# Six roundings of weights held behind the first layer, and the stores of raw weight quarters held back, in an attention and feed-forward kernel

## The chip, the cores and the metric

One core of one Trainium2 chip. The metric is the device time of one execution in microseconds (us), lower is better.

Engines are written as in the profile: PE (matrix multiplication), ACT, DVE, POOL (the three engines for elementwise work), and SP, which in this kernel issues nearly all transfers between DRAM and the chip. PSUM is the memory that PE's products go to; a bank is the part of it that one product takes up here. The granted clock is the share of full speed at which the profile shows PE's clock. L872 means line 872 of the kernel. **The change inserts four lines early on, so L872 of the kernel before is L876 in the changed kernel**, and so with all lines after the first inserted ones.

## The reference

```python
# q, k, v: (8, 8, 576, 64) float32;  w_ch1: (512, 2048), w_ch2: (2048, 512), both float64
q_s = softmax(q, axis=-1);  k_s = softmax(k, axis=2)
kv  = einsum('bhsd,bhse->bhde', k_s, v)
x   = einsum('bhsd,bhde->bhse', q_s, kv)          # -> (8, 576, 512), heads side by side
u   = x + real(fft2(x, axes=(1, 2)))
un  = (u - mean(u)) / sqrt(var(u) + 1e-6)         # over the last axis
out = u + maximum(un @ w_ch1, 0) @ w_ch2
```

(The two softmax lines stand for the reference's own six lines.) The weights arrive as float64, that is as pairs of 32-bit words, and the kernel rounds them to float32 itself.

## The kernel before

The kernel works through the token groups, and for each does attention, the Fourier mix, a normalisation and the two layers of the feed-forward block. For all groups but the first, the two layers are *split*: the weight matrices are cut into quarters, sums and differences of quarters are formed once (the *combination*), and seven products take the place of eight. The sums are stored to DRAM and read back. The first group cannot wait for that. It goes through *plain* layers, while the weights are still being rounded. This is the stretch from about 60 to 205 us, and the change lies entirely in it.

The weights are rounded in 32 blocks, 0 to 15 for the first layer and 16 to 31 for the second. Each block is loaded as 512 KB of words, and rounded by ACT, DVE, DVE, ACT and POOL in turn:

```python
def convert(i):
    pair = raws.pop(i).rearrange("p (n w) -> p n w", w=2)
    lo, hi = pair[:, :, 0], pair[:, :, 1]
    # ... cut: out is the block's place in the weights
    n = ("bc", "bb", "bc", "bb")[i] if i < 4 else "acc"
    if i < 20:
        t = self.ps.tile([P, 512], F32, tag=n, name=n, bufs=3 if i >= 4 else 1)[:]   # PSUM
    else:
        t = hi.bitcast(F32)                                                           # in place
    # ... cut
    nc.scalar.activation(t, hi.bitcast(F32), ACT.Copy, scale=2.0 ** -112)                            # L347
    V.tensor_scalar(out=to.bitcast(I32), in0=ti, scalar1=3, ..., op0=ALU.logical_shift_left)         # L348
    V.scalar_tensor_tensor(out=to.bitcast(I32), in0=ti, scalar=-(1 << 31), in1=to.bitcast(I32), ...) # L349
    nc.scalar.activation(lo, lo.bitcast(U32), ACT.Copy, scale=2.0 ** -29)                            # L352
    nc.gpsimd.tensor_tensor(out=out.bitcast(I32), in0=to.bitcast(I32), in1=lo, op=ALU.add)           # L353
```

There are only 14 places for words, so a block's words are overwritten by those of a later block. `WORDS_AT` gives the place of each block. The load of the later one is issued right behind the rounding of the earlier one, and waits for it:

```python
WORDS_AT = [*range(8), 8, 9, 10, *range(3, 8), 0, 1, 2, 8, 9, 10, 4, 5, 6, 7, 8, 11, 12, 7, 13, 8]
LATE_WORDS = (27, 28, 30)          # these have places of their own, and are loaded after the first layer

def round_blocks(some):
    for i in some:
        convert(i)
        if i in after:             # after[25] = 29, after[26] = 31, ...
            fetch(after[i])
```

The plain layers, and the order in which everything is issued around them:

```python
def up(f):                                     # first layer, block f of 16; three PSUM banks in turn
    n = ("ba", "bb", "bc")[f % 3]
    ph = self.ps.tile([P, 512], F32, tag=n, name=n)
    for k in range(KT):
        nc.tensor.matmul(ph[:], lhsT=self.w1sb[:, f, k * P:(k + 1) * P], rhs=..., ...)   # L872
    nc.scalar.activation(h[:, f, :], ph[:], ACT.Relu)                                    # L874
```
```python
round_blocks(range(1))
blk.gate(unT[:, 0, 0, :], blk.raws[NF][0:1, 0:2])
round_blocks(range(1, 4))
n = 2 * NF - 16
turn = [2 * i if i < 4 else 3 * i - 4 for i in range(12)]
for f in range(NF):                            # NF = 16
    up[f]()
    free(f)
    round_blocks(range(4 + n * f // NF, 4 + n * (f + 1) // NF))
rest = [lambda i=i: round_blocks([i]) for i in range(4 + n, 2 * NF)]
# ... cut: the steps of the combination; the loads of q; the words of LATE_WORDS
for i in range(len(down)):                     # the second layer, 64 steps on PE (L881)
    down[i]()
    if i in turn:
        rest[turn.index(i)]()
    # ... cut: a share of the combination, of the second batch's attention and of its transform
```

The second batch's attention runs between the matmuls of the second layer. The *q turn* is one step of it: PE transposes a tile of q (L613), ACT copies it out of PSUM (`qT`, L620), PE multiplies it by kv (L645), and ACT copies the result to x (L647). There are four such tiles.

Two helpers order work without moving data. `gate(t, raw)` is a DVE instruction of 1x2 elements (L490). It writes the first two words of `raw` back unchanged, but reads `t` too, so that nothing that uses `raw` can be placed ahead of what makes `t`. `hold` and `free(f)` do the same with tiny copies behind the relu of block `f`: the q loads may go out after block 12.

## Time and profile before

| | before |
|---|---|
| median of three runs | 1134.09 us (1133.23 to 1135.87) |
| span of the profiled execution (that run took 1136.19 us) | 1134.4 us |
| busy share of PE, DVE, ACT, POOL | 96%, 48%, 36%, 30% |
| second block of the first layer starts | 68.43 us |
| second layer starts | 129.71 us |
| split layers start | 204.44 us |

PE is the bound. The busy share of 96% is an average, however. The view that cuts the span into stretches tells where the other 4% lie. Its columns are: the stretch, its length, then the busy time and number of groups of PE, of its weight loads, of DVE, ACT and POOL, then the mean granted clock of PE, the share of the DMA engines and GB/s. Two stretches of the kernel before:

```profile
110.00:130.00 20.00, 12.79 (x25) 5.65 (x26) 6.99 (x15) 10.81 (x30) 4.99 (x7) 0.83 0.52 168
130.00:205.00 75.00, 73.01 (x271) 40.75 (x270) 52.24 (x115) 26.24 (x65) 35.36 (x38) 1.00 0.72 251
```

PE lost 7.2 us of the 20 us around block 13 and ran the rest at a granted clock of 0.83. In the second layer it lost 2.0 us of 75.

### The profile page before, as it was taken

What the parts mean: (1) busy time and instruction counts of PE and PEld (TensorE: products, weight loads), DVE (VectorE), ACT (ScalarE), POOL (GpSimd) and SP (SyncE); (2) the same over time, 40 slices, a digit from 0 to 9 for tenths busy, and PEclk for the clock granted to TensorE, in tenths of its full rate; (3) what the DMA queues carried; (4) which work ended last, traced back from release to release, by engine and by line L of the source; (5) the groups of instructions that cost most, each with busy time, mean ns of one, the idle gap of its engine ahead of it and who ended that gap; (6) DMA issues with size and microseconds to landing.
All of it is one profiled execution on the core that took longest, in us unless ns stands there. A gap on an engine that the chain in (4) does not pass through costs nothing.

```text
span 1134.4 us, 14587 instructions
## 1 busy us (share of the span) xinstructions
PE 1094.5 (96%) x5440; PEld 915.5 (81%) x5440; DVE 542.3 (48%) x1109; ACT 404.3 (36%) x975; POOL 335.3 (30%) x304
## 2 busy tenths in 40 slices
PE   5798899999999999999999999999999999999997
PEld 4643355888888988898889888888889888888886
DVE  6776586368433734375344733583434352203201
ACT  6694423355333513362325322442334152201200
POOL 2065382226103510334023402261034203302320
PEclk9999899999999999999999999999999999999999
DMA  9556668354346534544356335552453344434441
GB/s 304 174 200 186 231 218 303 116 206 176 111 151 220 185 142 145 194 157 176 127 176 220 149 102 179 193 200 107 144 193 148 116 156 156 182 143 156 151 186 55
DMA packets 92581, 193.79 MB, mean 171 GB/s; under 512 B 23120, under 2 KB 59728, under 8 KB 85344
## 3 DMA queue, kind: packets, MB, share of 16 engines
q1 hardware_dynamic: 90712, 191.82, 49.2%
q10 hardware_dynamic: 1800, 1.05, 0.3%
q8 instruction: 43, 0.70, 0.2%
q14 instruction: 26, 0.21, 0.1%
HBM read 168.72 MB, written 28.31 MB: 174 GB/s over the span
## 4 chain that ended last, share of the span: by engine, by line
PE 86%; ACT 4%; DMA 3%; DVE 3%; issue 2%; POOL 1%; ACTq 0%; SPq 0%; POOLq 0%; DVEq 0%
PE bb L942 15%; PE bb L980 15%; PE ba L942 10%; PE bc L980 10%; PE bc L942 10%; PE ba L980 10%; PE acc L563 3%; PE acc L645 2%; PE acc L738 2%; PE acc L741 2%; PE acc L762 2%; PE tr L613 1%; PE tr L842 1%; PE bc L881 1%; PE tr L549 1%
## 5 line engine op out<-in xcount | busy, mean ns | idle before, releaser
L942 PE MATMUL bb<-unT,big 128*128 128x256 f32 x768 | 187.4, 381 | 0.0
L980 PE MATMUL bb<-big 128*128 128x256 f32 x768 | 172.1, 379 | 0.0
L942 PEld LDWEIGHTS bb<-unT,big 128*128 128x128 f32 x768 | 142.8, 190 | 23.6 <-DVE u L910 2.6
L980 PEld LDWEIGHTS bb<-big 128*128 128x128 f32 x768 | 145.4, 190 | 20.3
L359 POOL TENSOR_TENSOR big<-big 128x512 f32<-128x512 f32 (+1 forms) x38 | 46.2, 1217 | 305.9 <-ACT big L954 305.9
L942 PE MATMUL bc<-unT,big 128*128 128x256 f32 x512 | 125.4, 379 | 0.0
L954 ACT ACTIVATE big<-big 128x512 f32<-128x512 f32 x96 | 60.3, 629 | 182.6 <-DVE big L953 182.1
L942 PE MATMUL ba<-unT,big 128*128 128x256 f32 x512 | 123.6, 379 | 0.2 <-ACT unT L846 0.2
L980 PE MATMUL bc<-big 128*128 128x256 f32 x512 | 116.0, 379 | 0.5 <-DVE x L997 0.5
L980 PE MATMUL ba<-big 128*128 128x256 f32 x512 | 114.8, 379 | 0.0
L914 DVE TENSOR_TENSOR u<-bb,s 128x512 f32<-128x512 f32 x40 | 27.6, 691 | 177.8 <-PE bb L980 120.4
L980 PEld LDWEIGHTS bc<-big 128*128 128x128 f32 x512 | 96.1, 190 | 14.3 <-DVE x L997 0.9
L980 PEld LDWEIGHTS ba<-big 128*128 128x128 f32 x512 | 95.7, 190 | 12.1
L942 PEld LDWEIGHTS bc<-unT,big 128*128 128x128 f32 x512 | 95.1, 190 | 12.6
L942 PEld LDWEIGHTS ba<-unT,big 128*128 128x128 f32 x512 | 95.1, 190 | 12.2 <-ACT unT L846 0.5
L367 POOL TENSOR_TENSOR unT<-unT 128x512 f32<-128x512 f32 x8 | 14.2, 1774 | 182.1 <-DVE unT L366 182.1
L602 ACT ACTIVATE q<-q,qm 128x64 f32<-128x64 f32 x240 | 61.6, 339 | 6.1 <-DVE qm L600 6.0
L910 DVE TENSOR_TENSOR u<-bb,s 128x512 f32<-128x512 f32 x40 | 27.6, 690 | 73.3 <-PE bb L942 38.7
L953 DVE TENSOR_TENSOR big<-bc,u 128x512 f32<-128x512 f32 x64 | 44.1, 689 | 22.8 <-PE bc L942 21.7
L992 POOL TENSOR_TENSOR x<-x,u 128x512 f32<-128x512 f32 x14 | 17.7, 1267 | 113.9 <-DVE u L914 101.3
L846 ACT COPY unT<-tr 128x512 f32<-128x512 f32 x36 | 20.7, 586 | 79.7 <-PE tr L842 79.1
L953 DVE TENSOR_TENSOR big<-bb,s 128x512 f32<-128x512 f32 x32 | 22.1, 690 | 55.6 <-PE bb L942 55.5
(248 smaller groups left out, 1653.9 us busy)
## 6 DMA issues: line engine op xcount, KB each, us to landing
big<-w1s SPq DMA_DIRECT2D x64, 896.0 KB
big<-w2s SPq DMA_DIRECT2D x56, 1024.0 KB
big<-in_w_dram SPq DMA_DIRECT2D x21, 512.0 KB
q<-in_q_dram SPq DMA_DIRECT2D x27, 256.0 KB
k<-in_kT_dram SPq DMA_DIRECT2D x24, 288.0 KB
v<-in_v_dram SPq DMA_DIRECT2D x24, 256.0 KB
words<-in_w_dram SPq DMA_DIRECT2D x8, 512.0 KB
mirror<-x SPq DMA_DIRECT2D x14, 256.0 KB
```

What stands on the lines that cost most here:

```text
L359: e1.tensor_tensor(out=to(4), in0=at(2), in1=at(3), op=ALU.add)
L563: nc.tensor.matmul(pk, lhsT=ks[:, c, :], rhs=v[:, c, :], start=(c == 0), stop=(c == NC - 1))
L602: nc.scalar.activation(heads[:, h, :], heads[:, h, :], ACT.Exp, bias=m[:, h:h + 1])
L645: nc.tensor.matmul(px[:, r * P:(r + 1) * P], lhsT=qT[:, r, :], rhs=self.kvr[b % 2][:, r, :], start=True, stop=True)
L738: nc.tensor.matmul(full[:, at:at + size], lhsT=t[:, own], rhs=self.ft[:, f + at:f + at + size], start=at == 0, stop=False, skip_group_chec ...
L741: nc.tensor.matmul(full[:, 0:NM], lhsT=g[:, tail], rhs=self.ft[:, f:f + NM], start=False, stop=True, skip_group_check=True)
L910: V.tensor_tensor(out=temp("u2"), in0=box["bb"][:], in1=box["s1"][:], op=ALU.add)
L914: V.tensor_tensor(out=temp("u3"), in0=box["bb"][:], in1=box["s1"][:], op=ALU.add)
L942: nc.tensor.matmul(bank()[:, i, :], lhsT=w[:, WA_AT[m], k * P:(k + 1) * P], rhs=unT[:, B_AT[m], k, :], start=first and i == 0 and k == 0, ...
L953: V.tensor_tensor(out=hp(i), in0=bank[:], in1=u[:], op=ALU.add)
L954: nc.scalar.activation(hp(i), hp(i), ACT.Relu)
L980: nc.tensor.matmul(bank()[:, i, :], lhsT=h[p][:, A_AT[m], i * P:(i + 1) * P], rhs=w[:, p, :], start=first and i == 0 and p == 0, stop=p == ...
```

## The change

The intent is to take the roundings that are not urgent out of the way of the first layer's relus. In the order of the code, 26 blocks instead of 20 are rounded by its end, with their halves through PSUM. The order on each engine is settled when the program is built, and differs: in the trace of the kernel before, POOL had finished 29 of the 32 blocks by then, all but 27, 28 and 30. So three roundings really leave the first layer, those of 26, 29 and 31. Block 26 is gated to the last relu, and blocks 27 to 31 to the first x of the second batch. The stores of raw quarters are held until block 12 by two tiny copies.

```diff
@@ free(f) @@
             for t in held.get(f, ()):
                 copy(t, self.h0[0:1, f, 0:1])
+            if f == 12:
+                for w in (self.w1sb[0:1, :, HD::HD], self.w2sb[0:1, 0:4, ::HD]):
+                    copy(w, w)
@@ convert(i) @@
-            if i < 20:
+            if i < 26:
@@ the first group @@
-            n = 2 * NF - 16
-            turn = [2 * i if i < 4 else 3 * i - 4 for i in range(12)]
+            n = 2 * NF - 10
             for f in range(NF):
                 up[f]()
                 free(f)
                 round_blocks(range(4 + n * f // NF, 4 + n * (f + 1) // NF))
+            blk.gate(blk.h0[:, NF - 1, :], blk.raws[26][0:1, 0:2])
+            turn = (0, 16, 19, 21, 23, 25)
@@ the second layer @@
                 down[i]()
+                if i == turn[1]:
+                    for n in range(27, 32):
+                        blk.gate(blk.xpart(1, 0, 0), blk.raws[n][0:1, 0:2])
                 if i in turn:
                     rest[turn.index(i)]()
```

## The prediction

> **What bounds the kernel now.** I read first the page's busy shares (the matmul engine is busy 96% of the span), then the waits of PE in two stretches, then PE, ACT and SP in order of time around the one large wait. From 205 us to the end PE waits for 2.4 us in all: nothing is to be gained there. From 60 to 205 us, where the first batch goes through the unsplit layers and the weights are rounded, the waits of PE are:
>
> ```profile
> PE bb L872 <- ACT big L874: 7.4, 1, 7.4
> PE acc L738 <- ACT ZT L749: 1.1, 1, 1.1
> PE ba L872 <- ACT unT L846: 1.0, 1, 1.0
> ...
> PE acc L645 <- ACT qT L620: 0.6, 1, 0.6
> ```
>
> Columns: total us, times, longest. One wait is 7.4 us. PE in order of time shows where it lies and what it costs besides:
>
> ```profile
> 102.77 3.60 PE L872 MATMUL bc<-unT,big 128*128 128x512 f32 x8
> 106.20 3.60 PE L872 MATMUL ba<-unT,big 128*128 128x512 f32 x8
> 117.21 5.80 PE L872 MATMUL bb<-unT,big 128*128 128x512 f32 x8 [7.41 <-ACT big L874]
> 122.84 3.60 PE L872 MATMUL bc<-unT,big 128*128 128x512 f32 x8
> 126.27 3.60 PE L872 MATMUL ba<-unT,big 128*128 128x512 f32 x8
> ```
>
> These are blocks 11 to 15 of the first layer (L872, three PSUM banks in turn). Block 13 could have started at 109.63 (106.20 + 3.43, the start-to-start time of the others), starts at 117.21 and takes 5.63 instead of 3.43. The second layer then begins at 129.71. Block 13 waits for its bank, which the relu (L874) of block 10 has to empty. That block's matmuls ended at 102.8, so I ask what ACT did instead:
>
> ```profile
> 101.12 0.58 ACT L874 ACTIVATE big<-ba 128x512 f32<-128x512 f32 x1
> 111.53 0.65 ACT L347 ACTIVATE big<-big 128x512 f32<-128x512 f32 x1 [9.82 <-DMA big<-in_w_dram]
> 112.09 0.66 ACT L352 ACTIVATE big<-big 128x512 int32<-128x512 uint32 x1
> 115.38 0.65 ACT L347 ACTIVATE words<-words 128x512 f32<-128x512 f32 x1 [2.63 <-DMA words<-in_w_dram]
> 115.94 0.66 ACT L352 ACTIVATE words<-words 128x512 int32<-128x512 uint32 x1
> 116.49 0.57 ACT L874 ACTIVATE big<-bb 128x512 f32<-128x512 f32 x1
> ```
>
> Two roundings stand ahead of the relu in ACT's order, and both wait for words from DRAM. Their loads, on the SP queue:
>
> ```profile
> 107.98 0.33 SPq L328 DMA_DIRECT2D big<-in_w_dram  x1
> 110.04 0.33 SPq L328 DMA_DIRECT2D words<-in_w_dram  x1
> ```
>
> By the places that the kernel gives to words these are blocks 29 and 31: each overwrites the words of blocks 25 and 26, whose last rounding steps on POOL end at 107.96 and 110.01. So work of the second layer (block 29 is first multiplied after 168 us) stands in front of a relu that PE needs at 109.6. It is an order, not a lack of capacity: ACT idles 9.8 us there.
>
> **What the Trainium skill says.** (1) "TensorE: Matmul & The Clock Gate", Architectural detail: the queues of ACT and DVE are strict FIFO, and PE alone pulls weight loads ahead. The trace agrees: the relu ran 13.7 us after its matmuls, right behind the two roundings. (2) The same page, Part 1 (The HAM clock gate): after an idle window of about 3.4 us the array runs at half clock until it has been busy for about as long. The trace agrees: block 13 took 2.20 us longer, and the mean granted clock from 109.8 to 129.7 was 0.83. So the wait costs more than its 7.4 us. (3) "SBUF — State Buffer", SBUF: two separate sides: DVE and GpSimd share a port pair under an exclusive lock, and the loser waits. (4) "VectorE: DVE Perf Modes", Why PSUM operands drop a tier: a PSUM operand rules the two-port mode out. The trace agrees on both: the shift (L348) took 686 ns on average from PSUM, but from 415 to 1509 ns from the words in SBUF, the long ones beside POOL.
>
> **The change part by part.** The order of the built programs shows PE's 864 rows unchanged; only ACT, DVE, POOL and SP differ.
>
> *Five gates of late words to the second batch's first x, and one of block 26 to the last relu.* Each is a DVE instruction of 1x2 elements, 0.14 us by those already there; six cost 0.9 us of DVE and nothing on the path. They do the work: in ACT's new order the relus of blocks 9 to 13 follow one another with no rounding between, block 26 stands behind the last relu, and 27 to 31 behind the first x copy (L647). What is then left from 109.63 to the second layer is three blocks of 3.43 = 10.29 us, against 129.71 - 109.63 = 20.08 now. **Saved: 9.8 us** (7.6 wait, 2.2 slow clock).
>
> *26 blocks instead of 20 with their halves through PSUM.* No instruction more. Blocks 20 to 25 read PSUM, 0.69 us per shift instead of about 1 us on average. ACT must now wait for one of three banks. By DVE's new order I place block 22 off its bank at about 99.2 (block 20 starts at 94.07 as now, since it needs POOL's block 18; then one copy that needs POOL's block 19, at 95.4; then six steps of 0.6). ACT then does block 25 and the relu of block 8 at about 100.5; PE needs that bank at 102.77. Slack 2.3 us: no wait.
>
> *The two copies of the held quarters.* 1x16 and 1x8 elements, 0.17 us each. The one on the first weights must follow the matmuls of block 12 that read the column (about 108.8), and block 13's third matmul must follow the copy; that matmul comes at 111.3, so 2 us are spare. The quarters' stores (8 of 128 KB) move from 87-96 us to about 109. They are wanted only when the split layer's weights are read back after 160 us: hidden. The q loads, gated to block 12's relu, go out at about 111 instead of 119.3.
>
> *Moved behind the first layer.* Blocks 26, 29 and 31 join 27, 28 and 30 in the second layer: three more roundings, each about 1.3 us of POOL, 1.1 of ACT, 1.1 of DVE, so 3.9, 3.4 and 3.4 us. POOL is busy 36 of the 74.7 us there, ACT 26, DVE 53: room, if the order is kind. Deadlines, 9.8 us earlier than now: block 26 at 148.4, 27 at 149.3, 28 at 158.8. Ready, estimated: first x copy 136.7, gates about 138.5, then ACT one block per 1.12 us and POOL one per 1.3: 27 at 141-142, 31 at 147-150. All in time; ACT's copies of later q and x for PE stand between these roundings, and may cost PE 0 to 1 us.
>
> *What the first layer's combination wins.* It starts with the last block of the first layer (127.58 now, so 117.8), and in POOL's new order blocks 27 and 28 no longer stand in its middle (141.58, 146.64), so it should end some 15 to 20 us earlier than now, the next keys' load goes out before 155 rather than at 165.8, and the 1.15 us wait at L738, which comes from those keys (landed 177.15) standing ahead of ZT on ACT, should vanish. I count 0.8 for it.
>
> Sum: 9.8 + 0.8 - 0.8 (new small waits, estimated) = 9.8 us; 1134.1 - 9.8 = **1124.3 us**.
>
> **Rivals.** (a) *The gain is given back in the second layer*: the chain of waits from 118 to 181 us runs through POOL, DVE and DMA, not PE, and ended with a PE wait already; with PE 9.8 us ahead and 3.9 us more of POOL work, that chain would keep up to 4-6 us. For it: that chain. Against: all of it starts at the end of the first layer too, and its POOL order gets better. It would make 1128 to 1130. (b) *Rounding through PSUM makes ACT wait for DVE in the first layer*: a relu of blocks 4 to 8 late by more than its slack, or PE held by the new copy. For it: ACT and DVE are 71% and 77% busy from 63 to 109.8. Each is worth 1 to 3 us: 1126 to 1127. (c) *The words held now arrive late and PE waits for block 26 or 27*: the slack is 7 us or more by my placing, but four chained estimates stand behind it; 1126 to 1132 if so. (d) *Everything fits and other waits go too*: the 0.6 us wait at L645 as well, 1122.
>
> **Range and chances.** Most weight lies on 1122 to 1126, with a tail upward from (a) and (c); the runs scatter by 2.6 us. Range 1121 to 1129.5. Two per cent are 22.7 us, over twice all that PE waits for in this stretch, so faster by that is all but excluded (0.01); slower by that would need the second layer to stall for over 30 us (0.02); within 0.97.
>
> **What would show it.** Right: PE has no wait over 1 us in L872 after its first block, block 13 takes 3.4 us, the second layer begins at 119.5 to 120.5, and the split layer (204.44 now) begins at 193 to 195.5. ACT's relu of block 10 starts within 1 us of its matmuls' end. The roundings 27 to 31 run from about 138 to 146 on ACT. Wrong: a new wait of PE for POOL's L353 group or for qT in the second layer (rivals a, c), a wait at L872 on DVE's copy or a late relu (b), or a first matmul of the split layer that waits for its loads.

## The result, and the profile after

| | before | after |
|---|---|---|
| median of four runs each, one chip | 1133.89 us (1133.23 to 1135.87) | 1129.21 us (1128.49 to 1129.27) |
| ratio | | 0.9954, 95% interval 0.9937 to 0.9972 |
| span of the profiled execution | 1134.4 us | 1126.7 us |

A ratio is the mean time of one kernel's fast runs over that of the other's fast runs of the same rounds, so it is not quite the ratio of the medians in the table. The change is 4.7 us faster by the medians. The time lies within the predicted range, 0.3 us below its upper end, but the gain is half of the 9.8 us that were worked out. The range held because of the tail that was left for rival (a), and not because of the sum.

The first layer behaved as foreseen. PE of the changed kernel in order of time, blocks 13 to 15 and the start of the second layer:

```profile
106.94 3.60 PE L876 MATMUL bb<-unT,big 128*128 128x512 f32 x8
110.37 3.60 PE L876 MATMUL bc<-unT,big 128*128 128x512 f32 x8
113.81 3.60 PE L876 MATMUL ba<-unT,big 128*128 128x512 f32 x8
117.24 3.60 PE L885 MATMUL bc<-big 128*128 128x512 f32 x8
```

Every block starts 3.43 us after the one before it. The 7.41 us wait is gone, and so is the slow clock behind it. ACT's relus of blocks 11 and 12 in the changed kernel show why:

```profile
103.71 0.60 ACT L878 ACTIVATE big<-bc 128x512 f32<-128x512 f32 x1 [2.83 <-PE bc L876]
107.14 0.60 ACT L878 ACTIVATE big<-ba 128x512 f32<-128x512 f32 x1 [2.84 <-PE ba L876]
```

ACT now waits for PE, and not PE for ACT: no rounding stands between these relus.

From 60 to 205 us the waits of PE in the changed kernel are (total us, times, longest):

```profile
PE acc L649 <- ACT qT L624: 4.4, 1, 4.4
PE ba L876 <- ACT unT L850: 1.0, 1, 1.0
...
PE acc L742 <- ACT ZT L753: 0.2, 1, 0.2
```

The wait for ZT has almost vanished, as foreseen (but not for the reason foreseen, see below). **The wait for qT, 0.6 us before, is now 4.4 us.** The stretches of the changed kernel that answer to those shown of before say the same:

```profile
110.00:130.00 20.00, 20.00 (x51) 9.09 (x50) 15.07 (x34) 11.21 (x36) 9.83 (x11) 1.00 0.66 226
130.00:205.00 75.00, 70.24 (x276) 43.50 (x275) 54.77 (x105) 25.82 (x58) 33.48 (x34) 0.98 0.69 238
```

PE is busy for all of the first 20 us at full clock. In the next 75 us it now loses 4.8 us instead of 2.0, and the clock falls to 0.98.

To add this up, I count from the start of the first layer's second block, whose matmuls are the same work at full clock in every run:

| stretch | before | after | difference |
|---|---|---|---|
| second block to second layer | 129.71 - 68.43 = 61.28 | 117.24 - 65.74 = 51.50 | -9.78 |
| second layer to split layers | 204.44 - 129.71 = 74.73 | 196.10 - 117.24 = 78.86 | +4.13 |
| split layers to the end | 1134.4 - 204.44 = 929.96 | 1126.7 - 196.10 = 930.60 | +0.64 |
| sum | 1065.97 | 1060.96 | -5.01 |

-5.0 us agrees with the medians (-4.7 here, -5.2 in a later repetition). The two profiled executions differ by 7.7 us. The other 2.7 us lie before the second block, 1.7 of them in the first block: it took 5.37 us in the one and 3.67 us in the other, for the same work. Over all profiles it took 5.37 us in six and 3.67 us in seven. Both kernels that I profiled twice showed the same value twice, and what decides between the two stayed open. I leave this part out of every comparison.

Next, the new wait. The changed kernel has several chains on several engines here. PE first, then ACT:

```profile
143.75 2.08 PE L649 MATMUL acc<-kvr,qT 128*128 128x128 f32 x8 [4.37 <-ACT qT L624]
145.62 1.06 PE L617 MATMUL tr<-ident,spare 128*128 128x128 f32 x4
```
```profile
139.32 0.67 ACT L351 ACTIVATE spare<-spare 128x512 f32<-128x512 f32 x1 [5.66 <-DVE spare L494]
...
142.66 0.56 ACT L651 COPY x<-acc 128x512 f32<-128x512 f32 x1
143.13 0.57 ACT L624 COPY qT<-tr 128x512 f32<-128x512 f32 x1
```

The cut lines are the other five steps of the roundings of blocks 27, 28 and 29. ACT idled 5.66 us until DVE had passed the gate (L494), then did three roundings, and only then the copy of qT that PE was waiting for. After the wait PE also ran at a slow clock: the two groups took 1.87 and 0.86 us from start to start, against 0.89 and 0.44 us at full clock. The excess is 0.98 + 0.42 = 1.40 us, and 1.46 with the next group.

DVE passed the gate at 139.14, though the x that it stands for was copied by ACT at 132.58 to 133.16. DVE had work of the combination ahead of it in its queue, and that waited for POOL. DVE, then POOL:

```profile
136.10 0.93 DVE L365 TENSOR_TENSOR big<-big 128x256 f32<-128x256 f32 x1 [1.98 <-POOL big L363]
...
139.14 0.21 DVE L494 SCALAR_TENSOR_TENSOR spare<-x,spare 1x2 int32<-1x2 int32 x2
```
```profile
125.67 1.36 POOL L357 TENSOR_TENSOR big<-big,words 128x512 int32<-128x512 int32 x1 [2.09 <-issue]
132.93 0.91 POOL L371 TENSOR_TENSOR s<-big 128x256 f32<-128x256 f32 x1 [5.89 <-issue]
```

POOL finished block 26 at 127.03, and then stood still for 5.89 us. Its next step overwrites the temporary `s`, which a store has to have read first. So the SP queue comes into it:

```profile
119.11 1.43 SPq L332 DMA_DIRECT2D spare<-in_w_dram  x3
127.06 0.33 SPq L332 DMA_DIRECT2D words<-in_w_dram  x1
127.44 0.43 SPq L409 DMA_DIRECT2D w1s<-u  x1
127.91 0.43 SPq L409 DMA_DIRECT2D w1s<-s  x1
```

Between 120.54 and 127.06 SP issued nothing. At its head stood the load of block 31's words, which overwrite those of block 26, and block 26 is now gated behind the last relu. That gate was late as well: the relu ended at 118.08, but DVE reached the gate only at 122.21, behind other work. The stores of `u` and `s` stood behind it. A load that nobody wants before some 20 us later held up the stores that the combination needs. This is the reading of one trace. The experiments test it.

### The profile page after: what moved, and what is told of

It is laid out like the page before. It is cut to its first block, busy times and chain, and to the rows that moved or that the text cites.

```text
span 1126.7 us, 14593 instructions
## 1 busy us (share of the span) xinstructions
PE 1092.0 (97%) x5440; PEld 917.6 (81%) x5440; DVE 542.3 (48%) x1117; ACT 404.6 (36%) x975; POOL 333.7 (30%) x304
## 4 chain that ended last, share of the span: by engine, by line
PE 84%; DVE 3%; issue 2%; POOL 2%; ACT 1%; DMA 0%; POOLq 0%; ACTq 0%; DVEq 0%
PE bb L946 15%; PE bb L984 15%; PE bc L984 10%; PE ba L984 10%; PE bc L946 10%; PE ba L946 10%; PE acc L567 2%; PE acc L649 2%; PE bc L885 2%; PE acc L766 1%; PE acc L742 1%; PE acc L745 1%; PE tr L846 1%; PE tr L617 1%; PE tr L553 1%
## 5 line engine op out<-in xcount | busy, mean ns | idle before, releaser
L946 PE MATMUL bb<-unT,big 128*128 128x256 f32 x768 | 187.4, 382 | 0.7 <-DVE u L918 0.7
L946 PEld LDWEIGHTS bb<-unT,big 128*128 128x128 f32 x768 | 143.2, 190 | 24.0 <-DVE u L914 2.6
L946 PE MATMUL bc<-unT,big 128*128 128x256 f32 x512 | 125.5, 380 | 0.0
L946 PE MATMUL ba<-unT,big 128*128 128x256 f32 x512 | 123.6, 380 | 0.2 <-ACT unT L850 0.2
L946 PEld LDWEIGHTS bc<-unT,big 128*128 128x128 f32 x512 | 95.4, 191 | 12.4
L946 PEld LDWEIGHTS ba<-unT,big 128*128 128x128 f32 x512 | 95.3, 191 | 12.0 <-ACT unT L850 0.5
```

What stands on the lines that cost most here:

```text
L946: nc.tensor.matmul(bank()[:, i, :], lhsT=w[:, WA_AT[m], k * P:(k + 1) * P], rhs=unT[:, B_AT[m], k, :], start=first and i == 0 and k == 0, ...
```

## The experiments

**Theory.** The new wait has two causes that add up. (1) The load of 31 holds SP, so the gates come late. (2) Once the gates open, three roundings of blocks that are not urgent stand on ACT ahead of qT. **Rivals**: the gates wait for DVE or POOL work anyway, whatever SP does; or the second layer is bound by the chain through POOL, DVE and DMA, so that the time would come back elsewhere (rival (a) of the prediction); or other parts of the change (more blocks by PSUM, the hold) cost something.

All runs agreed with the reference. In the table all times are medians. "Layer 1" is from the second block to the second layer, "layer 2" from there to the split layers, both from the profiles (us). The time before was 1134.58, 1134.79 and 1134.67 us in the three calls (11 runs each). Kernels of one call ran on one chip.

| call | kernel | us | ratio to before (95%) | layer 1 | layer 2 |
|---|---|---|---|---|---|
| | before (first profile) | | | 61.28 | 74.73 |
| | the change (first profile) | | | 51.50 | 78.86 |
| 1 | fetch31_later | 1127.32 | 0.9937 (0.9926 to 0.9949) | 51.50 | 76.61 |
| 1 | gates_alone | 1131.52 | 0.9977 (0.9966 to 0.9989) | 54.48 | 80.05 |
| 1 | hold_alone | 1134.64 | 1.0004 (0.9990 to 1.0018) | 60.90 | 73.24 |
| 1 | no_late_gates | 1132.12 | 0.9984 (0.9969 to 0.9999) | 53.37 | 80.40 |
| 2 | late_gates_last_x | 1130.06 | 0.9950 (0.9937 to 0.9963) | 51.50 | 78.95 |
| 2 | late_gates_last_x_sp_held | 1132.71 | 0.9980 (0.9967 to 0.9994) | 51.50 | 82.61 |
| 2 | no_gate_on_26 | 1129.15 | 0.9944 (0.9932 to 0.9956) | 52.32 | 79.49 |
| 2 | gates_29_31 | 1131.16 | 0.9968 (0.9953 to 0.9983) | 51.50 | 81.05 |
| 3 | last_x_all_at_once | 1125.89 | 0.9925 (0.9911 to 0.9938) | 51.50 | 76.35 |
| 3 | change_again | 1129.50 | 0.9959 (0.9945 to 0.9973) | 51.50 | 78.84 |
| 3 | fetch31_again | 1126.05 | 0.9928 (0.9915 to 0.9941) | 51.50 | 76.61 |

### 1. The load of block 31 issued later (fetch31_later)

The change, but the load of 31 is issued at step 12 of the second layer, behind the stores:

```diff
-            if i in after:
+            if i in after and after[i] != 31:
                 fetch(after[i])
@@ the second layer @@
                 down[i]()
+                if i == 12:
+                    fetch(31)
```

> The change, except that the load of block 31's words is issued at job 12 of the second layer instead of right after block 26's rounding. Theory (the load of 31 holds the SP queue from 120.5 to 127.1 us while it waits for block 26, the stores of the second quarter pair go out 6 us late, GpSimd's combination, VectorE's gates and ScalarE's roundings follow late, and PE waits 4.4 us for qT and loses 1.5 us more at a slow clock): GpSimd's wait of 5.9 us before the first L371 falls under 1.5 us, the gates run 4 to 5 us earlier, PE's wait for qT falls to under 1 us, and the time is 4 to 6 us under that of the change: 1123.5 to 1125.5. Rival 1 (the gates stand too late in VectorE's order whatever the stores do, behind the combination): the wait stays at 3 to 4.5 us and the time at 1128 to 1130. Rival 2 (GpSimd and VectorE simply have too much work there): the wait moves to another instruction, time 1127 to 1130.

POOL, DVE and PE of this kernel:

```profile
129.87 0.93 POOL L371 TENSOR_TENSOR s<-big 128x256 f32<-128x256 f32 x1 [0.62 <-DMA w1s<-s]
```
```profile
139.15 0.21 DVE L494 SCALAR_TENSOR_TENSOR spare<-x,spare 1x2 int32<-1x2 int32 x2
```
```profile
143.81 1.16 PE L649 MATMUL acc<-kvr,qT 128*128 128x128 f32 x8 [2.21 <-ACT qT L624]
144.81 0.82 PE L617 MATMUL tr<-ident,spare 128*128 128x128 f32 x4
145.42 3.40 PE L885 MATMUL ba<-big 128*128 128x512 f32 x4
```

POOL's wait fell from 5.89 to 0.62 us, so the place of that load was its cause. Two things came together: counted from the start of the second layer, the store of `s` was issued 3.6 us earlier (at +7.05 instead of +10.67), and POOL could go on 3.4 us after that instead of 5.0, now that no load of 512 KB had been issued just before. The gates opened 19.69 us after the start of the second layer (119.46) instead of 21.90, and the qT wait fell by as much, from 4.37 to 2.21 us. The expectation of a wait of 1 us or less was **missed**, and so was the time (1123.5 to 1125.5 expected, 1127.32 measured). DVE still did eight steps of the combination, from 134.97 to 139.15, ahead of the gates. The slow clock stayed too: the four matmuls at 145.42 take 1.88 us at full clock. So the theory holds for cause (1), at half of the wait.

### 2. The five gates alone (gates_alone)

The kernel before, with the five gates at step 16 and nothing else:

```diff
                 down[i]()
+                if i == 16:
+                    for n in range(27, 32):
+                        blk.gate(blk.xpart(1, 0, 0), blk.raws[n][0:1, 0:2])
```

> The kernel before plus only the five gates of the words of 27 to 31 (20 blocks rounded as before, no hold of stores, no gate on 26). Block 26 is rounded in the first layer here, so 31's load is not held and does not hold the SP queue. Theory (the wait at block 13 of the first layer comes from the roundings of 29 and 31 in front of a relu): that wait is gone, 9.8 us saved there; and no wait for qT over 1.5 us: 1123.5 to 1126, so better than the whole change. Rival (the other two parts are needed for the first layer): a wait of several us at L872 stays, 1129 to 1134. Rival (the gates themselves cost the qT wait): the first layer is clean but qT waits 3 to 4.5 us: 1128 to 1130.

The expectation was wrong. The wait at block 13 vanished (blocks 10 to 15 start 3.43 us apart), but two new waits came. PE of this kernel:

```profile
120.99 3.67 PE L881 MATMUL bc<-big 128*128 128x512 f32 x8 [2.82 <-POOL s L360]
...
147.69 2.08 PE L645 MATMUL acc<-kvr,qT 128*128 128x128 f32 x8 [4.47 <-ACT qT L620]
```

The second is the wait of the change itself. It came without the gate on block 26: here POOL waited 7.03 us for the store of `s`, which SP had issued at 128.40, behind the three loads of late words (1.5 MB, from 124.80). So the delayed store has more than one way to come about. The gates opened at 142.55, that is +21.56, nearly as late as in the change; run 7 shows what DVE has to do with that. The first wait lies at the end of the first layer. The view names POOL's step on `s`, which ended at 120.84. The relu of block 14, whose bank this matmul takes over, ended at 120.89 and fits as well; releasers are inferred, and this one stays undecided. The relu was late because the q loads went out late, at 112.32 instead of 107.94 in the change: the start of ACT's exponentials waited 5.40 us for them, and stood ahead of it. The rest of the change therefore does earn something in the first layer: 54.48 - 51.50 = 2.98 us. Whether the hold or the 26 blocks do that, this run doesn't tell.

### 3. The hold alone (hold_alone)

The kernel before, with the two copies of `free(12)` and nothing else:

```diff
+            if f == 12:
+                for w in (self.w1sb[0:1, :, HD::HD], self.w2sb[0:1, 0:4, ::HD]):
+                    copy(w, w)
```

> The kernel before plus only the two copies that hold the quarters' stores until block 12. The order of ScalarE still has the roundings of 29 and 31 in front of the relu of block 10. Theory: the wait at block 13 stays at 6 to 9 us, time 1132 to 1136. Rival (the stores before the loads on the SP queue made the loads late, as GB/s or as order): the wait falls by 3 us or more, time 1126 to 1131.

The copies cost and gain nothing that five rounds can show (1.0004, 0.9990 to 1.0018), as expected. (The second layer of its one profile is 1.5 us shorter than before, with a ZT wait of 0.38 us and none for qT; the medians show nothing of it.) The wait for block 10's relu is still there:

```profile
114.92 5.29 PE L876 MATMUL bb<-unT,big 128*128 128x512 f32 x8 [7.55 <-ACT big L878]
```

### 4. The change without the five late gates (no_late_gates)

```diff
-                if i == turn[1]:
-                    for n in range(27, 32):
-                        blk.gate(blk.xpart(1, 0, 0), blk.raws[n][0:1, 0:2])
```

> The change without the five gates of 27 to 31; the gate of 26, the hold and the 26 blocks stay. ScalarE's order now has half of block 29's rounding in front of the relu of block 10 and the rest behind it. Theory: 29's load goes out at about 103 us and lands about 4 us later, so the relu of block 10 is late by 1 to 4 us and PE waits 1 to 4 us in the first layer; in the second the roundings are no longer tied to the first x, so qT waits under 1.5 us: 1125 to 1129. Rival (the gates are what makes the first layer run free): a wait of 6 to 9 us at block 13, 1132 to 1135. Rival (the wait for qT comes from elsewhere than the gates): qT still waits over 3 us, 1130 or more.

The waits of PE from 60 to 205 us in this kernel, the three largest:

```profile
PE acc L742 <- ACT ZT L753: 3.5, 1, 3.5
PE acc L649 <- ACT qT L624: 2.1, 1, 2.1
PE bb L876 <- ACT big L878: 1.5, 1, 1.5
```

Without the gates layer 1 is 1.87 us longer than in the change, but 7.9 us shorter than before. So most of the gain in the first layer does not need the late gates, once 26 blocks are rounded and the 26th is gated: the prediction's "they do the work" gave the gates too much. With the gates alone (run 2) it was 6.8 us shorter. The two parts remove largely the same wait. In the second layer the gates are worth 1.54 us (80.40 - 78.86): without them 3.5 us at ZT appear, while the qT wait is 2.1 instead of 4.4 us. The expectation (1125 to 1129 us, a qT wait under 1.5 us) was **missed**.

### 5 and 6. Four of the gates moved to the last x (late_gates_last_x, late_gates_last_x_sp_held)

This tests cause (2). Only block 27 is gated to the first x. Blocks 28 to 31 are gated to the last, so that a single rounding stands ahead of qT. Run 5 also has the later load of 31, run 6 has not:

```diff
-            turn = (0, 16, 19, 21, 23, 25)
+            turn = (0, 16, 25, 27, 29, 31)
@@ the second layer @@
-                    for n in range(27, 32):
-                        blk.gate(blk.xpart(1, 0, 0), blk.raws[n][0:1, 0:2])
+                    blk.gate(blk.xpart(1, 0, 0), blk.raws[27][0:1, 0:2])
+                if i == 25:
+                    for n in range(28, 32):
+                        blk.gate(blk.xpart(1, 1, 1), blk.raws[n][0:1, 0:2])
```

> The change with the load of 31 moved as in fetch31_later, and with the gates of 28 to 31 on the last x of the second batch instead of its first (27 stays on the first). ScalarE's order has now one rounding, not three, in front of the third qT copy. Theory as mended (what is left of the wait, 2.2 us, comes from VectorE reaching the gates only behind eight combination steps, and from the three roundings in front of qT behind them): PE's wait for qT falls under 0.8 us, no slow clock after it, 1122.5 to 1125; the last blocks become tight, so up to 1.5 us of waits for POOL's L357 may appear in the second layer. Rival (the wait is set by the qT's own inputs or by PE's transposes): it stays near 2 us, 1126.5 to 1128.

> The change with only the gates of 28 to 31 moved to the last x; the load of 31 stands where the change has it and holds the SP queue. Theory (two causes in a row: SP's hold makes the gates late by 2.2 us, and three roundings of 1.12 us behind them stand in front of qT): the wait of 4.4 us falls by the two roundings taken away, 2.2 us, to 2 to 2.6 us, and the time to 1126 to 1128. Rival (only the roundings in front matter, SP's hold does not): under 0.8 us, and the same time as late_gates_last_x within 1 us. Rival (only SP's hold matters): 3.5 us or more, 1128.5 to 1129.5.

The qT wait of the four kernels makes a square:

| longest qT wait, us | three roundings ahead of qT | one rounding ahead |
|---|---|---|
| load of 31 holds SP | 4.37 (the change) | 2.11 (run 6) |
| load of 31 later | 2.21 (run 1) | none (run 5) |

Either cause alone is worth about 2.2 us, and both together the whole wait. Two roundings at 1.12 us are 2.24 us, and the gates' delay by SP was 2.21 us. The two-cause theory is shown for the wait. Both expected times were **missed** (1130.06 instead of 1122.5 to 1125, and 1132.71 instead of 1126 to 1128), and the second rival was right there. PE of run 5:

```profile
164.06 1.13 PE L885 MATMUL bc<-big 128*128 128x512 f32 x2 [2.30 <-POOL big L357]
165.02 4.43 PE L885 MATMUL bb<-big 128*128 128x512 f32 x6
```

Before this stood another wait of 1.64 us on the same line, and the six matmuls at 165.02 take 2.74 us at full clock. The waits are for the rounded blocks 30 and 31. POOL began their last steps at 158.86 and 162.55, behind the folds of the next transform. Time that the qT wait gave free was spent there.

### 7. No gate on block 26 (no_gate_on_26)

```diff
-            blk.gate(blk.h0[:, NF - 1, :], blk.raws[26][0:1, 0:2])
```

> The change without the gate on block 26 alone. Block 26 is rounded in the first layer again, so the load of 31 is free at about 104 us and never holds the SP queue: another way to take away the same suspect. Theory: GpSimd's wait before its first L371 falls under 2 us, PE's wait for qT to 1.5 to 3 us as in fetch31_later, the first layer keeps running without a wait, 1126 to 1128. Rival (block 26 was moved for a reason, its rounding in front of a relu stops the first layer): a wait of 1 us or more at L876 and 1128 or more. Rival (fetch31_later gained by chance or by another change of order): the qT wait stays at 4 us or more.

The time is that of the change. The qT wait is still 3.81 us. POOL of this kernel:

```profile
131.21 0.73 POOL L371 TENSOR_TENSOR s<-big 128x256 f32<-128x256 f32 x1 [6.19 <-DMA w1s<-s]
```

The expectations (a wait of POOL under 2 us, one for qT of 1.5 to 3 us) were **missed**. SP was free, and issued the store of `s` at 125.73, behind the three loads of late words (122.00) and the store of `u` (123.51). It landed 5.5 us later, beside the 1.5 MB of words. In run 1 the store was issued behind the same three loads, but landed in 3.4 us (126.51 to 129.87). That the words' traffic slowed it is argued from the overlap, and no run isolates it. POOL's wait is long here also because it starts earlier, as block 26 is out of its way. Counted from the start of the second layer, POOL's step on `s` came at +13.02, halfway between the change (+15.69) and run 1 (+10.41). But the gates gained only 1.0 us by that (+20.89, against +21.90 and +19.69). DVE did not wait for POOL: the same eight steps that took 4.18 us ahead of the gates in run 1 took 5.99 us here (133.09 to 139.08), and 6.01 us in run 2. POOL worked beside them for all but 0.8 us in both, and stood still for 2.5 us of them in run 1. The port lock of the prediction's point (3) would explain this; no run tests it. So the first rival, that the gates wait for DVE's work whatever SP does, is right in part.

### 8. Only blocks 29 and 31 gated (gates_29_31)

With the later load of 31:

```diff
-                    for n in range(27, 32):
+                    for n in (29, 31):
                         blk.gate(blk.xpart(1, 0, 0), blk.raws[n][0:1, 0:2])
```

> The change with 31's load moved and with gates only on 29 and 31, the two blocks that stood in front of the relu before; 27, 28 and 30 go where their words allow. ScalarE's order then has 27 and 28 before the fourth q's exponentials, 30 behind the first qT, and 29 and 31 in front of the third. Theory (each rounding in front of a qT copy costs its 1.12 us only if the gate is late): the wait at the third qT is 1 to 2 us and one at the first of up to 1.5 us, 1125 to 1128. Rival (the early words are what delays q and x): a wait over 2 us at the first qT, 1128 or more.

This was worse, and the expectation was **missed**. The roundings of 27 and 28, now free to start, took POOL's time ahead of the combination (132.34 and 135.52). POOL's step on `s` came at 137.72 instead of 129.87, the gates opened at 145.15, and PE waited 5.67 us for qT. Here an early start for work that isn't urgent delayed what is urgent in the same queue.

### 9 to 11. All at once after the last x; the change and run 1 again (last_x_all_at_once, change_again, fetch31_again)

Run 9 is run 5, with blocks 28 to 31 issued together right after their gates at step 25, so that their last steps on POOL should come ahead of the folds:

```diff
-            turn = (0, 16, 25, 27, 29, 31)
+            turn = (0, 16, 25, 25, 25, 25)
-                if i in turn:
-                    rest[turn.index(i)]()
+                for t, r in zip(turn, rest):
+                    if t == i:
+                        r()
```

> As late_gates_last_x, but blocks 28 to 31 are emitted together right after their gates, so that POOL's last steps of 30 and 31 (L357) stand ahead of the folds of the next layer and not behind them. If POOL's order alone made the 3.9 us of waits at L885 there, they vanish, qT waits 0, and the split layer begins 3 to 5 us earlier than in late_gates_last_x: 1125 to 1127.5. Rival: POOL and DVE have no room left in this stretch, so what no longer waits for a rounded block waits for the folds (a new wait of PE for eo or ZT of 2 us or more): 1128 to 1131.

> The change itself once more, on the same chip and in the same rounds as the other two, so that they can be compared directly. 1128.5 to 1129.5; qT wait of 4.4 us.

> The kernel of fetch31_later in the same rounds as the change. If the load of block 31 that holds the SP queue costs what the profiles say (2.2 us of the qT wait), it is 1.5 to 2.5 us faster than change_again: 1126.5 to 1127.5. If the earlier difference was scatter between calls, the two agree within 0.5 us.

The waits of PE in run 9, the two largest:

```profile
PE acc L742 <- DVE eo L710: 1.6, 1, 1.6
PE bc L885 <- POOL big L357: 1.3, 1, 1.3
```

The edit did only part of what was meant: of the six folds on POOL, one still stands ahead of the last step of block 30 (155.86) and four ahead of that of block 31 (160.40), where in run 5 all six stood ahead of both. The time came out as expected (1125 to 1127.5), the vanishing of the waits did not. The waits for rounded blocks fell from 3.9 to 1.3 us, and the slow clock behind them went, but a wait of 1.6 us for the folds (`eo`) took their place, as the rival of this run said, though smaller than its 2 us. Compared with run 5, layer 2 is 2.6 us shorter. What POOL's order alone is worth stays open.

In the same rounds, fetch31_again beat change_again by 3.4 us by the medians (1126.05 against 1129.50), more than the 1.5 to 2.5 us expected. The profiles show 78.84 - 76.61 = 2.23 us in layer 2. The rest is within the scatter of single runs, and 0.6 us of it may be the wait at L946 for DVE's `u`, which the change has (0.6 and 0.7 us) and this kernel has not. The intervals of the two ratios do not overlap.

**The version that beats both kernels** is the change with the load of 31 moved: 1127.32 and 1126.05 us. Run 9 is equal to it (1125.89). One line gives nearly the same as a new arrangement of the gates.

## Why the prediction was right or wrong, point by point

**Where the time is lost before: right.** The wait of block 13 was an order and not a lack of capacity: in the change PE is busy for the whole stretch in which it lost 7.2 us.

**Saved in the first layer, 9.8 us: right.** Measured 61.28 - 51.50 = 9.78 us, in both profiles of the change. This includes the slow clock's 2.2 us. (The second layer began at 117.24 and not at the 119.5 to 120.5 foreseen, because the second block had already begun 2.69 us earlier.) Which part earns it was put too simply: alone the five gates bring 6.80 us (run 2), but within the change they account for 1.87 us (run 4), since the 26 blocks and the gate on 26 remove most of the wait too.

**26 blocks through PSUM, the two copies: right.** No wait of PE came from them (rival (b) did not occur). ACT did wait 2.40 and 1.15 us for DVE at the banks (94.41 and 96.80), as the prediction had allowed for. The copies measured nothing (run 3). The q loads went out at 107.94, 9.3 us before the second layer; 9.0 had been estimated (111 against 120.0).

**What the combination wins: the numbers fit, the reason does not.** The next keys' load went out at 153.55 (predicted: before 155), and the wait at ZT fell by 0.99 us (counted: 0.8). But counted from the start of the second layer that load went out at +36.31, against +36.10 before: the combination won nothing beyond the layer's earlier start, where 5 to 10 us more had been foreseen. ZT itself was ready later (its copy on ACT began at +55.60, against +51.47). PE waited less for it only because PE came later too, after the qT wait and the slow clock. In runs 5 and 9, with next to no qT wait, that copy also began later than before (+52.21 and +52.51). So it is luck that this term came out. The 0.6 us at the kernel before's L645 went as well, as rival (d) had it; it is gone with the hold alone, too (run 3).

**Moved behind the first layer: this step failed.** The term "0.8 (new small waits, estimated)" measured 4.37 us of waiting and 1.46 us of slow clock behind it, 5.83 us in all. The working shows where. "First x copy 136.7, gates about 138.5" was for a second layer starting at 120.0, so the gates were to open 18.5 us after that start. They opened 139.14 - 117.24 = 21.90 us after it, though the x that they read was there earlier than foreseen (133.16, or +15.92, against +16.7). A new wait for qT was one of the prediction's own signs of being wrong. The rest of the step held: ACT did take 1.12 us per block, and the copies of qT do stand between the roundings. To cost nothing the gates would have had to open 4.37 us earlier, at +17.53. At the predicted +18.5 the wait would have been 1.0 us, just the "0 to 1 us" of the text. The 3.4 us by which the gates were late, and the slow clock, are the miss. Of the 3.4 us, 2.21 are SP's hold (run 1, both times); the remaining 1.2 us is DVE's own queue, where steps of the combination stand ahead of the gates (eight in run 1, done without a pause; six in the change). I had placed the gates by the x that they read and not by what stands before them in DVE's queue. And I had asked of every moved block when it is *needed*, but not what its *load* holds up while it waits to be issued.

The slow clock was an omission of its own. The prediction says of the old wait that it "costs more than its 7.4 us", and then gives the new waits no such surcharge.

**The sum** with the measured terms: -9.78 (first layer) - 0.99 (ZT) - 0.60 (the old qT wait) + 4.37 + 1.46 = -5.54 us up to the split layers, against -5.65 in the profiles. After these, 0.64 us more gives -5.0.

**The rivals.** (a) named the right mechanism, a second layer bound by the chain through POOL, DVE and DMA that ends in a wait of PE, and its time (1128 to 1130) is the one that was measured. It was given too little weight: the argument against it, that the chain starts earlier too, is right for its POOL part, but the gate on 26 had delayed the chain's store. Runs 5 and 9 show how tight this chain is, and so does run 1: ZT's copy begins there at +52.92, and PE takes it up at +53.70. (c), late words, did not occur in the change, but did in run 5.

## What to carry to other kernels

When you delay work to clear an in-order queue, follow what the delayed work itself holds: its load sits in the transfer queue, and everything issued behind that load waits too (here one 512 KB load, wanted by nobody for 20 us, cost 2.2 us, and moving it won them back). A gate opens when its own engine gets to it, not when the value it reads is ready, and several pieces of work behind one gate come out as a burst that stands in front of whatever else that engine owes PE. When a large wait of PE is removed, price each new wait with a clock penalty as well, and look for the next chain that runs through the other engines before counting the whole wait as gain.

## What the Trainium skill lacked or had wrong

- "TensorE: Matmul & The Clock Gate", Part 1 (The HAM clock gate) puts the fall to half clock after an idle window of about 3.4 us, and calls the window free-running. Here the clock fell after waits of PE of 2.11, 2.21 (twice) and 2.30 us (runs 6, 1, 11 and 5; the last with another of 1.64 us shortly before it), and did not fall after one of 2.82 us (run 2). The length of a gap alone did not decide, and a gap of 2.1 to 2.3 us cannot hold a whole idle window of 3.4 us wherever the window begins. After 2.21 us it also fell late: the first eight matmuls after the gap ran at nearly full speed (1.00 us from start to start, against 0.89), and the four from 145.42 took 3.40 instead of 1.88 us. A free-running window would fit such a delay, but no run here tests it. (The ends of matmuls are modelled in the profile, so the gaps may be off by a little.)
- "DMA: Bandwidth & Descriptors", Queues, rings and completion order tells in which order transfers complete. What decided is the order of issue, on which that section has nothing, and no other page says outright what stands behind a transfer that waits: a load on SP that waited for a buffer kept the stores behind it from being issued, from 120.54 to 127.06 us, and moving that one load took POOL's wait from 5.89 to 0.62 us.
